# Sparse attention and a routed expert layer on one core: masks in another order, two stores moved, the last expert's pairs swapped, the fallback flag read earlier

## The chip, the cores and the metric

The kernel runs on 1 core of a Trainium2 chip. A time is the device time of one execution of the program in microseconds (us); a kernel's time is the median of its runs. The core has a matrix engine (PE; its weight loads are listed apart as PEld), a vector engine (DVE), a scalar engine (ACT), a general engine (POOL, which also issues the indirect DMAs here) and SyncE (SP, which issues the plain DMAs). Every engine works through its own instruction queue in order and waits on semaphores that the others raise.

## What is computed

An attention layer over 8 batches, 8 heads, 576 positions and head size 64, in float32, is followed by an expert layer on its output.

```python
mask_local = (rel >= 0) & (rel < 32)                       # heads 0 to 3
mask_strided = (rel >= 0) & (pos[None, :] % 32 == pos[:, None] % 32)   # heads 4 to 7
attn = softmax(where(mask, scale * q @ k.T, -1e9)); x = attn @ v       # (8, 576, 512)
...
logits = x @ w_gate                                        # 8 experts
for b in range(B):
    for s in range(S):                                     # fresh choice, or that of s - 1
        e = fresh_e if s == 0 or local_gate[b, s] < 0.5 else prev_e
        out[b, s] = p[e] * (relu(x[b, s] @ w1[e]) @ w2[e])   # 512 -> 1024 -> 512
```

## The kernel before, in words

The order of the work is written out by hand (`manual_schedule`): what the Python code emits first is first in each engine's queue.

**Attention** (`attention`, from line 143). A unit of work is a batch and a pair of heads; there are 32, in the order batch, then local pair, local pair, strided pair, strided pair. Each pair has two halves. A step n of the main loop emits for pair n the scores (PE, line 252) and the exponential (ACT, line 256), for local pairs the product with the mask `maskL` (DVE, line 263; strided pairs add their mask `maskS` by a matmul, line 246), and for pair n - 1 the product with the values (PE, line 276) and the normalization (DVE, lines 289 and 290). So in step n = 1 PE's queue holds the scores of pair 1 and behind them the values of pair 0. Before the loop all constants are made: `maskL` on POOL (lines 184 to 190), then in a loop over two sizes the two parts of `maskS`, the first 126 wide and the second 72 wide (lines 193 to 215: a chain of small DVE operations with some on POOL), then `fold`, `down`, `pos8` and `start` (lines 217 to 230). The first strided pair is pair 2. The list `also[n]` holds callables that are emitted at the end of step n.

**Routing** (`Router`). For batches 0 to 3 the choice of experts, the counts and the slot of each row are worked out during the attention, for batches 4 to 7 at the start of the expert stage. A row's number and its gate (8 bytes) are written to a table `slots` in DRAM by indirect DMAs on POOL, 20 for each half (`scatters`, line 577). `fetch` (line 643) reads the table back into `tab`, and `table` (line 647) makes the row numbers `gi`. `arms` also works out `pick`, for each expert which of 7 code arms it needs, and `flag` (line 676), which is positive when the fast path does not hold.

**Experts** (`Experts.run`). The rows of an expert are handled in pairs of tiles of 128 rows. A pair's first layer, `pair_hidden`, has 7 products of 16 matmuls (line 807; one level of a Strassen scheme, whose sums are on DVE, line 795). Its second layer, `pair_output`, has 7 products of 8 (line 843) and two indirect stores of 128 rows to `out`, `scatter` (line 763). `gather` (line 737) fetches the rows of a coming pair, `scale` and `turn` (lines 743, 750) multiply by the gate and transpose them, in the middle of the pair before. `steps` and `places` are lists of callables that `run(steps)` emits at marked points inside a pair; the first such point of `pair_hidden` lies behind its second product. The first two pairs (`self.first` of expert 0, `other` of expert 1) are known early. During the first one the second routing is emitted, whose 20 slot scatters stand in POOL's queue with the two stores of the first pair among them.

An expert may have more rows than its two pairs take. `choose(e)` (lines 960 to 965) loads `pick[e]` into a register of PE, ACT, DVE and POOL and gives a prefetch hint for the arms. `rest` runs the second pair of the expert up to the middle of its second layer, branches (`tc.Switch`, line 975), and finishes the pair in the arm, followed by the further tiles: none, a half tile of 64 rows (`half`, lines 919 to 941), a whole one (`single`, lines 898 to 910), both, and so on. For experts 1 and 0 `choose` stands ahead of the layer; for experts 2 to 7 it stands between the first pair's `pair_hidden` and its `output`. For expert 7 nothing follows the arm but the end.

**The end.** After the expert stage `values_load(flag)` (line 118) loads the flag into a register of all five engines, and `tc.If(redo > 0)` (line 120) holds a slow general version of the whole program, which is skipped on this input.

Part of `pair_output` with the stores that are moved:

```python
            def part2(nxt, steps):
                ...
                add(y[:, 1, 256:], v3, vb)
                self.scatter(y, 1, r)
                self.turn(nxt, bank)
                run(steps)
                ...
                add(y[:, 0, 256:], v4, va)
                self.scatter(y, 0, r)
```

Of the kernel before, what the change touches and what calls it, by code (L numbers as in the profile page):

```python
# [93 lines left out]
@with_exitstack  # L94
def attention_then_scomoe(ctx: ExitStack, tc: tile.TileContext, qkl, qks, vl, vs, wg, q, k, vl2, vs2, wg2, w1, w2, out):
    nc = tc.nc
    dram = ctx.enter_context(tc.tile_pool(name="dram", bufs=1, space=DRAM))
    xd = dram.tile([N, D], F32, name="xd")
    keep = ctx.enter_context(tc.tile_pool(name="keep", bufs=1))
    ident = keep.tile([P, P], F32, name="ident")  # L100
    make_identity(nc, ident)

    with ExitStack() as fast:
        once = fast.enter_context(tc.tile_pool(name="once", bufs=1))
        router = Router(once, dram, tc, ident)
        one = Weights(once)
        spot = (once.tile([P, 2, D], F32, name="x0"), once.tile([P, 2, DK, P], F32, name="xt"),
                once.tile([P, 4, 2, P], F32, name="tt"))
        with tc.manual_schedule():
            moe = Experts(nc, tc, xd, w1, w2, out, ident, router, one, spot)  # L110
            with ExitStack() as part:
                attention(part, tc, qkl, qks, vl, vs, wg, xd, ident, router, moe)
            with ExitStack() as part:
                moe.run(part)
        flag = router.flag


    redo = nc.values_load(flag, min_val=0, max_val=P + N,
                          skip_runtime_bounds_check_because="a count of at most 128 rows and of pairs")
    with tc.If(redo > 0):  # L120
        with ExitStack() as slow:
            general(slow, tc, q, k, vl2, vs2, wg2, w1, w2, xd, out, ident)

# [19 lines left out]
def attention(ctx, tc, qkl, qks, vl, vs, wg, xd, ident, router, moe):  # L143
# [46 lines left out]
    nc.gpsimd.memset(maskL[0:STRIDE, 0], 0.0)  # L190

    maskS = consts.tile([GK, 2 * GK + GL], BF16, name="maskS")
    for n, c in ((GK, GC), (GL, GR)):
        i = consts.tile([GK, n], I32, name=f"i{n}")
        cls = consts.tile([GK, n], F32, name=f"cls{n}")
        div = consts.tile([GK, n], F32, name=f"div{n}")
        both = []
        for mult, pattern in ((1, [[0, n]]), (0, [[1, n]])):

            nc.gpsimd.iota(i, pattern=pattern, base=0, channel_multiplier=mult)  # L200
            t = consts.tile([GK, n], F32, name=f"cls{n}{mult}")
            nc.vector.tensor_copy(t, i)
            nc.vector.tensor_scalar(i, i, 65536 // c + 1, None, Alu.mult)
            nc.vector.tensor_scalar(i, i, 16, None, Alu.arith_shift_right)
            nc.vector.tensor_copy(div, i)
            nc.vector.scalar_tensor_tensor(t, div, -float(c), t, Alu.mult, Alu.add)
            both.append(t)
        nc.vector.tensor_tensor(cls, both[0], both[1], op=Alu.not_equal)
        nc.vector.tensor_scalar(cls, cls, NEG, None, Alu.mult)
        nc.gpsimd.affine_select(out=cls, in_=cls, compare_op=Alu.is_ge, fill=NEG, base=0, pattern=[[1, n]],  # L210
                                channel_multiplier=-1)
        if n == GK:
            nc.vector.tensor_copy(maskS[:, 0:2 * n].rearrange("p (a x) -> p a x", a=2), across(cls, [n, 2, n]))
        else:
            nc.vector.tensor_copy(maskS[:, 2 * GK:], cls)

    fold = consts.tile([P, E + 1], F32, name="fold")
    nc.vector.tensor_reduce(fold, ident.rearrange("p (k x) -> p x k", k=DK)[:, 0:E + 1], axis=AX.X, op=Alu.add)


    ci = consts.tile([P, E], I32, name="ci")
    nc.gpsimd.iota(ci, pattern=[[-1, E]], base=E, channel_multiplier=0)
    down = consts.tile([P, E], F32, name="down")
    nc.vector.tensor_copy(down, ci)
    pi = consts.tile([P, CH], I32, name="pi")
    nc.gpsimd.iota(pi, pattern=[[E * P, CH]], base=E, channel_multiplier=E)
    pos8 = consts.tile([P, CH], F32, name="pos8")
    nc.vector.tensor_copy(pos8, pi)
    start = consts.tile([P, CH], F32, name="start")
    nc.vector.tensor_scalar(start, pos8, float(E), None, Alu.is_equal)  # L230

    def spans(u):

# [160 lines left out]
        u.n = n  # L394

    also = {n: [] for n in range(len(units) + 3)}
    also[2] = [router.constants]
    n = PAIRS * RB + 3
    turn, scan, hot, count, slot, back = router.steps(0, bank)
# [327 lines left out]
class Experts:  # L727
# [41 lines left out]
    def run(self, ctx):  # L769
# [66 lines left out]
        def pair_output(r, w, h):  # L836
# [25 lines left out]
                nc.scalar.copy(out=y[:, 0, 0:256], in_=va)  # L862
                run(steps)

            def part2(nxt, steps):
                self.scale(nxt)
                prod(k2, t[2], qb)
                add(v2, q1, vb)
# [17 lines left out]

# [65 lines left out]

            return [[todo.pop(0) for _ in range(min(n, len(todo)))] for n in counts]

        def output(r, w, h, nxt, steps):
            part1, part2 = pair_output(r, w, h)
            part1(steps)
            part2(nxt, steps)

        def choose(e):  # L960
            value = nc.values_load(router.pick[0:1, e:e + 1], engines=ENG, min_val=0, max_val=ARMS - 1,
# [2 lines left out]
            tc.switch_hint(index, ARMS, label=f"expert{e}")  # L964
            return index

        def rest(e, w, spot, second, index, steps, nxt):

            if nxt is not None:
                self.gather(nxt)  # L970
            part1, part2 = pair_output(second, w, pair_hidden(second, w, steps))
            part1(steps)
            flip = state["flip"]

            for arm in tc.Switch(index, ARMS, hint=f"expert{e}"):
# [22 lines left out]
                while left:  # L998
                    run(left)


        sums = load(1, W[1])
        other = Rows(spots[1], *self.early, [1, EARLY + 1], RB * S)
# [20 lines left out]
        index = choose(0)  # L1024
        sums = load(2, W[1])
        nxt = rows(0, 2, (0, 1))
        rest(0, W[0], 1, second, index, slots(sums, [0, 0, 1, 2, 1, 2, 2, 2, 2]) + [[f] for f in sums], nxt)
        for e in range(2, E):
            w, first, steps = W[(e + 1) % 2], nxt, []
            second = rows(1, e, (2, 3))  # L1030
            self.gather(second)
            if e + 1 < E:
                steps = slots(load(e + 1, W[e % 2]), [0] * 5 + [1, 1, 1, 3] + [1] * 8 + [2])
                nxt = rows(0, e + 1, (0, 1))
            else:
                nxt = None
# [3 lines left out]
            rest(e, w, 1, second, index, steps, nxt)  # L1040


def shifted_attention(ctx, tc, q, k, vl, vs, wg, xd, ident, probs, codes):
# [460 lines left out]
```

## Time and profile before

| | |
|---|---|
| runs | 739.37, 734.49, 740.71 us; median 739.37 |
| the profiled execution | 738.92 us, its span 737.2 us, mean granted TensorE clock 0.959 |
| busy, share of the span | PE 683.0 us (93%), PEld 586.5 (80%), DVE 353.4 (48%), ACT 195.5 (27%), POOL 134.7 (18%) |
| stages | attention 0 to about 199 us, first pair of the experts 199 to 229, pair `other` of expert 1 229 to 269, all others 269 to 725, end 725 to 737.2 |
| arm of expert 7 in this run | one whole tile and one half tile |

How to read it: the span is the time from the first instruction to the last. A line of the timeline has the start, the duration, the engine, the line of the kernel, the operation with its tiles, and in brackets how long the engine had been idle and what ended that. A line of the chain of waits has the start, the duration and what the end of the program waited for at that time; "issue" is time that nothing in the profile explains, "another core or an unknown queue" (in the timeline "remote") a wait that ended at a time at which no engine of the profile had just finished. `POOLq` and the like are rows of an engine's sequencer, such as branches and register loads, which do not count as busy.

### The profile page before, as it was taken

What the parts mean: (1) busy time and instruction counts of PE and PEld (TensorE: products, weight loads), DVE (VectorE), ACT (ScalarE), POOL (GpSimd) and SP (SyncE); (2) the same over time, 40 slices, a digit from 0 to 9 for tenths busy, and PEclk for the clock granted to TensorE, in tenths of its full rate; (3) what the DMA queues carried; (4) which work ended last, traced back from release to release, by engine and by line L of the source; (5) the groups of instructions that cost most, each with busy time, mean ns of one, the idle gap of its engine ahead of it and who ended that gap; (6) DMA issues with size and microseconds to landing.
All of it is one profiled execution on the core that took longest, in us unless ns stands there. A gap on an engine that the chain in (4) does not pass through costs nothing.

```text
span 737.2 us, 14832 instructions
## 1 busy us (share of the span) xinstructions
PE 683.0 (93%) x6034; PEld 586.5 (80%) x6034; DVE 353.4 (48%) x843; ACT 195.5 (27%) x357; POOL 134.7 (18%) x150
## 2 busy tenths in 40 slices
PE   7999999497899699999999999999999999999992
PEld 5878887385698589985998899999589899789961
DVE  6568766272466534451463265455126646524300
ACT  2544443141321122212222123122322222222210
POOL 3000001405127330221121120221012012111010
PEclk9999999597699899999999999999999999999997
DMA  9797887731360022615321711720171262010010
GB/s 325 275 328 267 279 286 256 249 84 52 95 228 30 3 86 67 238 38 173 109 74 47 254 47 50 251 73 21 39 257 59 76 210 66 32 37 30 18 50 13
DMA packets 37803, 95.33 MB, mean 129 GB/s; under 512 B 5230, under 2 KB 14446, under 8 KB 37632
## 3 DMA queue, kind: packets, MB, share of 16 engines
q1 hardware_dynamic: 29616, 73.77, 29.0%
q0 software_dynamic: 7488, 19.56, 8.4%
q8 instruction: 66, 1.08, 0.6%
q14 instruction: 105, 0.86, 0.4%
q10 hardware_dynamic: 528, 0.07, 0.1%
HBM read 74.41 MB, written 19.49 MB: 127 GB/s over the span
## 4 chain that ended last, share of the span: by engine, by line
PE 79%; issue 7%; DVE 5%; DMA 3%; another core or an unknown queue 3%; ACT 1%; POOL 1%; SPq 0%; DVEq 0%; POOLq 0%; ACTq 0%
PE mps L843 26%; PE lps L807 25%; PE vps L276 5%; PE sps L252 4%; PE tps L317 3%; PE lps L898 3%; PE mps L909 3%; PE xps L750 2%; DMA w1t<-in_w_dram 2%; PE mps L935 2%; PE lps L919 1%; PE sps L246 1%; PE tps L336 1%; PE vps L354 1%
## 5 line engine op out<-in xcount | busy, mean ns | idle before, releaser
L763 POOL DMA_INDIRECT out_dram<-y,tab x40 | 45.5, 1138 | 323.9 <-DVE y L795 217.4
L807 PE MATMUL lps<-tt,ws 128*128 128x128 f32 x768 | 91.5, 275 | 0.4 <-issue 0.2
L807 PEld LDWEIGHTS lps<-tt,ws 128*128 128x128 f32 x768 | 88.5, 192 | 0.8 <-DVE u L795 0.4
L843 PE MATMUL mps<-wt,k 128*128 128x256 f32 x384 | 85.6, 379 | 0.0
L843 PEld LDWEIGHTS mps<-wt,k 128*128 128x128 f32 x384 | 72.9, 190 | 9.9
L577 POOL DMA_INDIRECT slots<-tok,idx x40 | 40.9, 1023 | 147.5 <-DVE tok L568 135.9
L807 PE MATMUL lps<-xt,w1t 128*128 128x128 f32 x512 | 64.8, 281 | 2.6 <-ACT y L941 1.4
L807 PEld LDWEIGHTS lps<-xt,w1t 128*128 128x128 f32 x512 | 62.1, 196 | 6.1 <-ACT y L941 2.8
L795 DVE TENSOR_TENSOR h<-lps,u 128x512 f32<-128x512 f32 x48 | 33.2, 691 | 66.5 <-PE lps L807 57.3
L843 PE MATMUL mps<-w2t,h 128*128 128x256 f32 x256 | 61.3, 383 | 0.0
L737 POOL DMA_INDIRECT x<-xd,gi x40 | 40.4, 1009 | 112.5 <-PE lps L807 34.9
L252 PE MATMUL sps<-qk 64*128 64x96 f32 (+2 forms) x704 | 55.4, 288 | 4.9 <-issue 4.1
L252 PEld LDWEIGHTS sps<-qk 64*128 64x128 f32 (+2 forms) x704 | 45.5, 188 | 14.8 <-issue 12.5
L256 ACT ACTIVATE e<-sps 128x576 f32<-128x576 f32 (+1 forms) x64 | 41.2, 651 | 58.4 <-PE sps L252 40.8
L843 PEld LDWEIGHTS mps<-w2t,h 128*128 128x128 f32 x256 | 48.1, 193 | 6.0
L794 ACT ACTIVATE h<-h 128x512 f32<-128x512 f32 x48 | 30.3, 630 | 75.5 <-DVE h L795 71.7
L794 ACT ACTIVATE h<-lps 128x512 f32<-128x512 f32 x28 | 16.5, 594 | 86.8 <-PE lps L807 58.8
L795 DVE TENSOR_TENSOR u<-lps,p 128x512 f32<-128x512 f32 x16 | 11.1, 692 | 57.9 <-PE lps L807 32.3
L807 PE MATMUL lps<-xt,ws 128*128 128x128 f32 x256 | 33.1, 285 | 6.0 <-DVE h L795 6.0
L743 ACT ACTIVATE x<-x,tab 128x512 f32<-128x512 f32 (+1 forms) x40 | 27.2, 718 | 40.6 <-DMA x<-xd,gi 26.9
L807 PEld LDWEIGHTS lps<-xt,ws 128*128 128x128 f32 x256 | 31.5, 201 | 6.2 <-DVE h L795 6.2
L276 PE MATMUL vps<-vl,e 128*64 128x65 f32 x768 | 29.4, 235 | 7.0 <-issue 4.7
(222 smaller groups left out, 977.4 us busy)
## 6 DMA issues: line engine op xcount, KB each, us to landing
w1t<-in_w_dram SPq DMA_DIRECT2D x8, 2048.0 KB
w2t<-in_w_dram SPq DMA_DIRECT2D x8, 2048.0 KB
qk<-in_qkl_dram SPq DMA_DIRECT2D x16, 592.0 KB
qk<-in_qks_dram SPq DMA_DIRECT2D x16, 576.0 KB
vl<-in_vf_dram SPq DMA_DIRECT2D x8, 780.0 KB
vs<-in_vg_dram SPq DMA_DIRECT2D x8, 639.8 KB
xd<-xl SPq DMA_DIRECT2D x16, 288.0 KB
xd<-xs SPq DMA_DIRECT2D x64, 63.0 KB
```

Of the source, the lines that this page charges most:

```text
L252: nc.tensor.matmul(ps[0:m, h, c:c + w], lhsT=t[r, S + j * width:S + j * width + m], rhs=t[r, j * width:j * width + w], start=(u.local and ...
L256: nc.scalar.activation(e[0:kb, :, 0:n], ps[0:kb, :, 0:n], Act.Exp, bias=0.0, scale=1.0 / DH ** 0.5)
L276: nc.tensor.matmul(ps[a * HALF:(a + 1) * HALF, h, i], lhsT=u.e[0:m, h, q0:q0 + HALF], rhs=vt[0:m, j, 2 * i2 + h], start=(i == 0 and h == 0 ...
L317: nc.tensor.transpose(ps[:, t], src[:, t], ident)
L577: s = self.nc.gpsimd.indirect_dma_start(out=self.T, out_offset=bass.IndirectOffsetOnAxis(ap=self.idx[0:m, t, b:b + 1], axis=0), in_=self.t ...
L737: self.nc.gpsimd.indirect_dma_start(out=r.x[0:r.m, i], out_offset=None, in_=self.xd[0:r.rows], in_offset=bass.IndirectOffsetOnAxis(ap=r.gi ...
L743: self.nc.scalar.activation(r.x[0:r.m, i], r.x[0:r.m, i], Act.Copy, scale=r.gate[i][0:r.m])
L763: s = self.nc.gpsimd.indirect_dma_start(out=self.out, out_offset=bass.IndirectOffsetOnAxis(ap=r.si[i][0:r.m], axis=0), in_=y[0:r.m, i], in ...
L794: relu = lambda o, i: nc.scalar.activation(o, i, Act.Relu)
L795: add = lambda o, i, p: nc.vector.tensor_tensor(o, p, i, op=Alu.add)
L807: nc.tensor.matmul(ps[:, f], lhsT=m[:, kk, f * P:(f + 1) * P], rhs=v[:, kk], start=(start and f == 0 and kk == 0), stop=(kk == 1), skip_gr ...
L843: nc.tensor.matmul(ps[:, 0:256], lhsT=m[:, f], rhs=v[:, f], start=(start and f == 0), stop=(f == 3), skip_group_check=True)
```

## The change

- Only the first part of `maskS` is made ahead of the loop. The second part is emitted at the end of step 0, the other small constants at the end of step 1.
- The two stores of the first pair are kept in a list and emitted behind `router.fetch()`, so in POOL's queue behind all 20 slot scatters and the fetch.
- For experts 1, 0 and 7 `choose` becomes the first step inside `pair_hidden`, behind its second product.
- For expert 7 the pair with tiles 0 and 1 goes through `rest` (with the switch and the further tiles), and the pair with tiles 2 and 3 comes behind the switch.
- The flag is loaded inside the first layer of that last pair. The `If` has another block as its fall-through: in the program the empty branch now lies directly behind the compare, and the general version behind it is jumped over; before, the general version lay directly behind the compare and the empty branch behind that.

```diff
-        flag = router.flag
-    redo = nc.values_load(flag, min_val=0, max_val=P + N, ...)
-    with tc.If(redo > 0):
+                redo = moe.run(part)
+    with tc.If(redo > 0, preferred_fallthrough_block=False):
...
-    for n, c in ((GK, GC), (GL, GR)):
+    def classes(n, c):
...
+    classes(GK, GC)
     fold = consts.tile([P, E + 1], F32, name="fold")
-    nc.vector.tensor_reduce(fold, ...)
+    def more_constants():
+        nc.vector.tensor_reduce(fold, ...)
...
+    also[0] = [lambda: classes(GL, GR)]
+    also[1] = [more_constants]
     also[2] = [router.constants]
...
-            def part2(nxt, steps):
+            def part2(nxt, steps, late=None):
+                send = self.scatter if late is None else lambda *a: late.append(lambda: self.scatter(*a))
...
-                self.scatter(y, 1, r)
+                send(y, 1, r)
...
-                self.scatter(y, 0, r)
+                send(y, 0, r)
...
-        def rest(e, w, spot, second, index, steps, nxt):
-            if nxt is not None:
-                self.gather(nxt)
-            part1, part2 = pair_output(second, w, pair_hidden(second, w, steps))
+        def rest(e, w, spot, pair, steps, nxt, index=None):
+            self.gather(nxt)
+            if index is None:
+                steps = [[lambda: chosen.append(choose(e))]] + steps
+            part1, part2 = pair_output(pair, w, pair_hidden(pair, w, steps))
             part1(steps)
+            index = index or chosen.pop()
...
-        output(self.first, W[0], pair_hidden(self.first, W[0], places), other, places)
+        late = []
+        output(self.first, W[0], pair_hidden(self.first, W[0], places), other, places, late)
...
         router.fetch()
+        for do in late:
+            do()
         output(other, W[1], h, second, places)
...
-        rest(1, W[1], 0, second, choose(1), [], nxt)
+        rest(1, W[1], 0, second, [], nxt)
...
-        for e in range(2, E):
+        for e in range(2, E - 1):
...
+        second = rows(0, e + 1, (2, 3))
+        rest(e + 1, W[e % 2], 1, nxt, [], second)
+        check = lambda: chosen.append(nc.values_load(router.flag, ...))
+        output(second, W[e % 2], pair_hidden(second, W[e % 2], [[check]]), None, [])
+        return chosen.pop()
```

More of the change, by code (lines that the diff above doesn't have):

```diff
@@ L113, in attention_then_scomoe @@
             with ExitStack() as part:
-                moe.run(part)
-        flag = router.flag
-    redo = nc.values_load(flag, min_val=0, max_val=P + N,
-                          skip_runtime_bounds_check_because="a count of at most 128 rows and of pairs")
-    with tc.If(redo > 0):
+                redo = moe.run(part)
+    with tc.If(redo > 0, preferred_fallthrough_block=False):
         with ExitStack() as slow:
@@ L215, in attention @@
             nc.vector.tensor_copy(maskS[:, 2 * GK:], cls)
+    classes(GK, GC)
     fold = consts.tile([P, E + 1], F32, name="fold")
-    nc.vector.tensor_reduce(fold, ident.rearrange("p (k x) -> p x k", k=DK)[:, 0:E + 1], axis=AX.X, op=Alu.add)
     ci = consts.tile([P, E], I32, name="ci")
-    nc.gpsimd.iota(ci, pattern=[[-1, E]], base=E, channel_multiplier=0)
     down = consts.tile([P, E], F32, name="down")
-    nc.vector.tensor_copy(down, ci)
     pi = consts.tile([P, CH], I32, name="pi")
-    nc.gpsimd.iota(pi, pattern=[[E * P, CH]], base=E, channel_multiplier=E)
     pos8 = consts.tile([P, CH], F32, name="pos8")
-    nc.vector.tensor_copy(pos8, pi)
     start = consts.tile([P, CH], F32, name="start")
-    nc.vector.tensor_scalar(start, pos8, float(E), None, Alu.is_equal)
+    def more_constants():
+        nc.vector.tensor_reduce(fold, ident.rearrange("p (k x) -> p x k", k=DK)[:, 0:E + 1], axis=AX.X, op=Alu.add)
+        nc.gpsimd.iota(ci, pattern=[[-1, E]], base=E, channel_multiplier=0)
+        nc.vector.tensor_copy(down, ci)
+        nc.gpsimd.iota(pi, pattern=[[E * P, CH]], base=E, channel_multiplier=E)
+        nc.vector.tensor_copy(pos8, pi)
+        nc.vector.tensor_scalar(start, pos8, float(E), None, Alu.is_equal)
     def spans(u):
@@ L953, in slots, with output @@
             return [[todo.pop(0) for _ in range(min(n, len(todo)))] for n in counts]
-        def output(r, w, h, nxt, steps):
+        def output(r, w, h, nxt, steps, late=None):
             part1, part2 = pair_output(r, w, h)
             part1(steps)
-            part2(nxt, steps)
+            part2(nxt, steps, late)
         def choose(e):
@@ L999, in rest @@
                     run(left)
+        chosen = []
         sums = load(1, W[1])
@@ L1019, in run @@
         router.fetch()
+        for do in late:
+            do()
         output(other, W[1], h, second, places)
         nxt = rows(1, 0, (2, 3))
-        rest(1, W[1], 0, second, choose(1), [], nxt)
+        rest(1, W[1], 0, second, [], nxt)
         second = nxt
-        index = choose(0)
         sums = load(2, W[1])
         nxt = rows(0, 2, (0, 1))
-        rest(0, W[0], 1, second, index, slots(sums, [0, 0, 1, 2, 1, 2, 2, 2, 2]) + [[f] for f in sums], nxt)
-        for e in range(2, E):
-            w, first, steps = W[(e + 1) % 2], nxt, []
+        rest(0, W[0], 1, second, slots(sums, [0, 1, 2, 1, 2, 2, 2, 2]) + [[f] for f in sums], nxt)
+        for e in range(2, E - 1):
+            w, first = W[(e + 1) % 2], nxt
             second = rows(1, e, (2, 3))
             self.gather(second)
[L1032 to L1036, printed above, removed]
+            steps = slots(load(e + 1, W[e % 2]), [0] * 5 + [1, 1, 1, 3] + [1] * 8 + [2])
+            nxt = rows(0, e + 1, (0, 1))
             h = pair_hidden(first, w, steps)
@@ L1039, in run @@
             output(first, w, h, second, steps)
-            rest(e, w, 1, second, index, steps, nxt)
+            rest(e, w, 1, second, steps, nxt, index)
+        second = rows(0, e + 1, (2, 3))
+        rest(e + 1, W[e % 2], 1, nxt, [], second)
+        check = lambda: chosen.append(nc.values_load(
+            router.flag, min_val=0, max_val=P + N,
+            skip_runtime_bounds_check_because="a count of at most 128 rows and of pairs"))
+        output(second, W[e % 2], pair_hidden(second, W[e % 2], [[check]]), None, [])
+        return chosen.pop()
 def shifted_attention(ctx, tc, q, k, vl, vs, wg, xd, ident, probs, codes):
```

## The prediction

> **What bounds the kernel now.** I read the page first, then the table of stages (the busy time of each engine in chosen stretches), then for each place that the change touches the timeline, and for the end the sequencer's rows by line.
>
> ```profile
> span 737.2 us, 14832 instructions
> PE   7999999497899699999999999999999999999992
> PEclk9999999597699899999999999999999999999997
> ```
>
> PE is busy in nine tenths or more of most slices. What is left stands in a few places. The columns of the next view are the stretch, its length, then for each engine busy us and instructions, then the granted PE clock, the DMA share and GB/s.
>
> ```profile
> 8.40:11.80 3.40, 1.58 (x24) 1.45 (x24) 2.74 (x15) 1.38 (x3) 1.43 (x9) 1.00 1.06 307
> 11.80:15.20 3.40, 2.83 (x49) 2.71 (x49) 3.18 (x6) 0.00 (x0) 1.90 (x7) 0.50 0.99 370
> ...
> 126.00:143.00 17.00, 6.71 (x72) 4.88 (x70) 2.65 (x11) 0.62 (x3) 10.61 (x11) 0.65 0.80 244
> ...
> 170.00:199.00 29.00, 20.38 (x210) 15.56 (x211) 7.03 (x27) 7.56 (x15) 11.16 (x12) 0.71 0.30 80
> ...
> 243.10:249.00 5.90, 0.00 (x0) 0.00 (x0) 0.70 (x2) 0.15 (x1) 3.78 (x4) 0.86 0.02 1
> ...
> 247.30:254.10 6.80, 5.06 (x20) 4.79 (x21) 5.57 (x16) 1.26 (x2) 0.98 (x1) 0.50 0.06 8
> ...
> 700.00:737.00 37.00, 23.59 (x142) 14.88 (x140) 1.12 (x2) 4.01 (x9) 4.80 (x5) 0.89 0.10 32
> ```
>
> PE loses time at 8 to 15 us, in three stretches in which POOL is the busy engine (126 to 143, 170 to 199, 233 to 254), and at the end. Between 269 and 700 it is busy for 425.8 of 431 us, so little can be won there. The change touches the first, the last of the three stretches, and the end.
>
> **Part 1, masks.** In the timeline of the start:
>
> ```profile
> 8.50 1.58 PE L252 MATMUL sps<-qk 64*128 64x96 f32 x24 [0.72 <-ACT e L256]
> 11.57 2.76 DVE L263 TENSOR_TENSOR e<-e,maskL 128x576 f32<-128x576 f32 x4
> 12.37 2.87 PE L276 MATMUL vps<-vl,e 128*64 128x65 f32 x48 [2.29 <-DVE e L263]
> 17.35 0.87 PE L317 MATMUL tps<-ident,xl 128*128 128x128 f32 x6
> ```
>
> PE has done the scores of pair 1 at 10.08 and waits 2.29 for DVE, which works on the second mask (7.64 to 11.04) and small constants (to 11.57) before it masks pair 0, whose exponentials are ready at 8.48. After: DVE masks pair 0 by 9.2 (two operations of 0.7), so PE starts the values at 10.08, 2.29 earlier. What is late next: DVE makes the second mask from 9.2 to 12.6 (3.4, as before), masks pair 1 to 14.0, then does the four norm operations of pair 0 (0.2 and 0.56 each, 1.6 in all) to 15.6; PE's transposes, which began at 17.35, wait for those. Net 1.8 earlier. The small constants (0.6 on DVE) come next, ahead of the norm of pair 1, for which PE's values take 1.6 anyway. The second mask is done at 12.6 and PE needs it then for pair 2. On POOL the clearing of `sums` (0.46) moves ahead of two index rows that DVE takes at 9.2 or later: nothing. The loads follow PE's progress, and DMA is at 0.57 of its time from 27 to 36, so the shift should pass on. Bounds: 2.3 (the whole wait), and 0.1 if the new gap of about 1.6 before the transposes halves the clock for one stretch of 3.4 (1.7 lost). I take 1.8: PE is busy for more than 2 of the 3.4 us there, more than in the row 8.40:11.80, after which the clock halved.
>
> The Trainium skill's page "TensorE: Matmul & The Clock Gate", section "What's actually happening", puts the clock at half after an idle window of about 3.4 us. The rows above go against it in part: 1.58 busy of 3.40 was enough to halve it. By the page alone the gap of 1.6 costs nothing and the start gains 1.8 for certain; by the rows 0.1 stays possible.
>
> **Part 2, stores behind the slots.** The chain of waits and the timeline at the third stretch:
>
> ```profile
> 235.22 3.03 another core or an unknown queue
> 240.16 8.11 another core or an unknown queue
> ```
>
> ```profile
> 232.33 0.98 POOL L763 DMA_INDIRECT out_dram<-y,tab  x1 [0.31 <-issue]
> 245.77 0.92 POOL L577 DMA_INDIRECT slots<-tok,idx  x1 [0.30 <-issue]
> 248.08 0.98 POOL L643 DMA_DIRECT2D tab<-slots  x1 [1.40 <-DMA slots<-tok,idx]
> 248.30 0.69 DVE L795 TENSOR_TENSOR h<-lps,u 128x512 f32<-128x512 f32 x1 [8.13 <-remote]
> 249.04 3.78 PE L807 MATMUL lps<-xt,ws 128*128 128x128 f32 x16 [5.97 <-DVE h L795]
> ```
>
> DVE waits for a product whose matmuls began by 238.8, yet goes on at 248.30, 1.6 after POOL's last slot scatter (246.69). The two earlier stretches end alike: scatters end at 139.9 and 181.9, the engines go on at 142.5 and 183.1. So the profile ties the release to the end of the unbroken row of scatters; what holds PE's completions it does not show. The two stores stand in this row at 228.24 (1.17 and a pause of 0.30) and 232.33 (0.98 and 0.30). Without them the last scatter ends 2.75 earlier, and by the rule of the three stretches the release too. I take 2.75. The clock: PE works 249.0 to 254.1 at half, a loss of 2.5; with the idle stretch 2.75 shorter I expect one stretch of 3.4 at half, a loss of 1.7, so 0.8 more. What stands behind: the fetch goes out at 245.3, the stores end by 248.9, and the gathers behind them wait for DVE's `gi` (before: 259.79), so they are not held. `gi` needs the table, now read 2.75 earlier.
> Bounds: the pair's first layer took from 229.34 to 252.82, 23.5, where the next takes 12.5. If the stores cause the stretch (it sets in right behind them, and eight scatters from 216.2 to 228.2 held nobody), all 11.0 goes. If instead the release waits for the whole row of POOL's DMAs, now with the stores (to 248.9) behind the fetch, it comes at 250.5: 2.2 lost. The other two stretches had no stores among their scatters, which is why I stay with 2.75.
>
> **Part 3, choices inside the layer.** Before, DVE and ACT come back from expert 1's arm at 300.2 and 298.1, load the register (0.33 and 0.39) and then work on a product that is ready; PE waits 0.21 for DVE at 301.7. After, the load (with its hint 0.9) stands behind that work, ahead of `u3`, which PE needs two products later (3.6). Gain 0.2. Bounds: 0.6 (13.1 from 294.4 to 307.5 against 12.5), and 1.0 lost if PE's own load (0.32, with its hint 0.96) drains its queue in the middle of a layer; the nearest row, between two layers, shows no gap, hence 0.2. The flag's load is one such row (0.3) per engine and as well covered.
>
> **Part 4, the end.** The sequencer's rows of POOL, by line (name, times in ns, first and last start in us):
>
> ```profile
> L118 POOLq TENSOR_LOAD <-flag x1: 312/312/312, 730.2 to 730.2; - x1
> L120 POOLq EVENT_SEMAPHORE  x5: 17/42/43, 733.3 to 733.6; - x5
> L120 POOLq INC_SWDGE_SEM  x1: 642/642/642, 733.7 to 733.7; - x1
> L1500 POOLq COMPARE_BRANCH  x1: 45/45/45, 726.6 to 726.6; - x1
> ```
>
> PE ends at 725.07. The last store starts at 726.16; POOL leaves the arm at 726.7 and has its next instruction at 730.2: 3.55 for the jump. Flag 0.4, jump over the general version 2.6 (to 733.3), waits for the stores 0.4, queue count 0.64, then 2.8 to 737.2. From the store's start: 11.04.
> After: no arm to leave, no flag to load. But the empty branch now comes before the jump: the wait for the store's landing (2.7 after its start for 128 rows: 702.32 to 705.04) is no longer beside it. From the store's start: 2.7 + 0.4 + 0.64 + jump 2.6 + 2.8 = 9.2. From PE's end to that start: one DVE sum 0.42 and 0.3 instead of two ACT copies, 0.75 for 1.09. Tail 2.2 shorter.
> In PE's work the same matmuls stand. The half tile's gap of 0.70 at 719.3 is filled by the next pair's transposes, as at 643.9 (1.02, against 0.87 where they stood). The gap of 0.79 stays. New is one join: PE waits 0.47 after a half tile (650.3, 537.3), and the layer behind it takes 12.77 or 13.1 for 12.5, since ACT and DVE come back late; 0.74 to 1.07. Net 0.3 lost; part 4 gains 1.9. Bounds: 3.7 (the landing is beside the jump after all) and 0.3 lost (a join whose returns cost the whole 2.2 more; the slowest return, POOL's 6.3, does not hold PE).
>
> **The sum.** 1.8 + 2.75 + 0.8 + 0.2 + 1.9 = 7.45. From the profiled execution's 738.92: 731.5. That execution lies 0.45 below the median of 739.37. A measurement of this kernel tells about 1% from no change.
>
> **The rivals.**
> A, the stores cause the third stretch: 11.0 instead of 3.55, so 738.92 - 1.8 - 11.0 - 0.2 - 1.9 = 724.0. For it: the onset right behind the stores. Against: the two other stretches.
> B, the release waits for POOL's whole row of DMAs: 2.2 lost instead of 3.55 won, 737.2. For it: gathers (169.5 and 170.8) stand ahead of the second stretch, so it need not be the 8-byte scatters alone. Against: POOL pauses 1.4 for the landing before the fetch, and before, the release came in that pause.
> C, slower: the join behind expert 7's arms. If the code pages of the engines come one behind the other (1.7 + 5.3 + 5.8 + 6.0 = 18.8 from the rows at 291 to 303) PE waits some 13.8 more than now (ACT's return matters from about 5 on), 745.3 or more. It makes the kernel slower from a return of 12.4 on. Against: seven joins of the profile, none above 6.3.
>
> **How the numbers follow.** The forecast (728.5 to 734.5) has 0.53, A 0.17, B 0.22, C 0.08. Faster by over 1% is below 732.0: all of A and 0.33 of the forecast, 0.50. Slower by over 1% is above 746.8: most of C, 0.06. The rest, 0.44, lies within 1%. The range takes A and B in: 722 to 738.5 leaves out the lower end of A and C.
>
> **What would show it.** Right: PE's values at 10.1; DVE's product behind the scatters some 2.7 earlier against its pair's start, the two stores behind the fetch; no POOL jump of 3.5 behind the last store, and its queue count before the last jump. Wrong: half clock between 15 and 19; PE idle until the stores are out (B) or not at all (A); ACT or DVE more than 6 us away after expert 7's arm.

## The result, and the profile after

In a comparison of 20 executions each on the same chips the changed kernel takes 733.18 us (730.52 to 739.49) and the kernel before 737.24 (732.62 to 741.38). The ratio is 0.9945, with a 95% interval of 0.9925 to 0.9966: 4.1 us gained (2.5 to 5.5), where the prediction summed up 7.45. The profiled execution of the changed kernel took 733.33 us, 5.6 less than that of the kernel before.

The head of its page, and the table of stages (stretch, its length, busy us and instructions of PE, PEld, DVE, ACT and POOL, granted PE clock, DMA share, GB/s):

```profile
span 731.5 us, 14839 instructions
PE   8999998597898899999999999999999999999993
PEclk9999999597799799999999999999999999999998
```

```profile
8.40:11.80 3.40, 3.39 (x74) 3.10 (x74) 3.07 (x13) 1.42 (x3) 0.19 (x1) 1.00 1.06 315
11.80:15.20 3.40, 2.39 (x26) 1.71 (x25) 2.94 (x9) 1.30 (x2) 2.72 (x13) 1.00 1.02 384
126.00:143.00 17.00, 7.95 (x71) 5.13 (x74) 4.52 (x14) 1.79 (x4) 8.11 (x9) 0.56 0.84 242
170.00:199.00 29.00, 22.21 (x181) 17.45 (x182) 9.78 (x41) 7.16 (x15) 8.66 (x9) 0.66 0.24 64
231.00:237.10 6.10, 3.54 (x26) 3.05 (x25) 1.89 (x3) 0.00 (x0) 4.86 (x5) 1.00 0.02 1
237.10:247.40 10.30, 7.98 (x35) 7.56 (x35) 4.69 (x8) 1.50 (x3) 6.07 (x6) 0.50 0.18 57
```

The start has changed: PE is busy for all of 8.4 to 11.8, and the stretch behind it runs at full clock (from 15.2 to 18.6 too, with PE busy for 3.32 of 3.40). The two stretches of the attention are there as before. So is the third: PE works 3.54 of 6.10 us from 231, and then it is at half clock for 10.3 us, where it was 6.8 before.

The timeline of the start:

```profile
7.88 1.43 DVE L263 TENSOR_TENSOR e<-e,maskL 128x576 f32<-128x576 f32 x2
9.92 1.62 PE L276 MATMUL vps<-vl,e 128*64 128x65 f32 x48
12.42 0.20 DVE L212 CAST maskS<-cls 126x72 bf16<-126x72 f32 x1 [0.35 <-POOL cls L207]
12.54 1.42 DVE L263 TENSOR_TENSOR e<-e,maskL 128x576 f32<-128x576 f32 x2
14.80 1.15 PE L317 MATMUL tps<-ident,xl 128*128 128x128 f32 x6 [0.87 <-DVE sums L289]
```

DVE masks pair 0 at once, PE's values start at 9.92 (12.37 before), the second mask is done at 12.62, and the transposes begin at 14.80 (17.35).

The third stretch, where `other` (expert 1's first pair) begins at 226.02. "Release" is the time at which the engines behind PE go on again:

```profile
234.06 0.69 DVE L797 TENSOR_TENSOR u<-lps,p 128x512 f32<-128x512 f32 x1 [6.15 <-remote]
239.06 0.91 POOL L579 DMA_INDIRECT slots<-tok,idx  x1 [0.30 <-issue]
241.35 0.97 POOL L645 DMA_DIRECT2D tab<-slots  x1 [1.39 <-DMA slots<-tok,idx]
241.84 0.69 DVE L797 TENSOR_TENSOR u<-lps,u 128x512 f32<-128x512 f32 x1 [5.88 <-remote]
242.59 3.77 PE L809 MATMUL lps<-tt,w1t 128*128 128x128 f32 x16
242.63 1.37 POOL L765 DMA_INDIRECT out_dram<-y,tab  x1 [0.30 <-DVE u L797]
244.31 1.47 POOL L765 DMA_INDIRECT out_dram<-y,tab  x1 [0.30 <-issue]
246.16 2.53 PE L809 MATMUL lps<-xt,ws 128*128 128x128 f32 x16
```

The last scatter ends at 239.97 and the engines go on at 241.84, before the two stores are out. So the release has come 6.5 us earlier, 3.1 of it against the start of its pair. But DVE had already waited 6.15 for the sum before, and PE still has two products to do behind the release, both slowed by the half clock (3.77 and 2.53). Before, it had one.

The end, POOL's sequencer rows at the last store (it starts at 721.61) and behind it, by line (name, shortest, median and longest in ns, first and last start):

```profile
L117 POOLq EVENT_SEMAPHORE  x5: 17/43/3267, 721.5 to 721.8; - x5
L117 POOLq COMPARE_BRANCH  x2: 48/54/60, 721.4 to 725.8; - x2
L117 POOLq INC_SWDGE_SEM  x1: 635/635/635, 725.1 to 725.1; - x1
```

```profile
L1514 POOLq DRAIN  x3: 44/112/2039, 728.6 to 731.3; - x3
```

No jump stands behind the last store any more: the compare is at 721.4, 3.27 us go into the wait for the landing, then the queue count, and only then the second branch (725.8), behind which nothing comes until 728.6.

Where the 5.7 us between the two spans lie, read from the start times of the same matmuls in both: 2.27 at the start, 1.05 at a wait before the transposes at 54.40, 0.42 in pair `other`, 0.67 in the layer behind expert 1's arm, 0.26 in small pieces, 0.44 at expert 7's choice, 0.40 lost at its join, 0.97 behind PE's end. The wait of 0.99 at 54.40 belongs to none of the parts for certain: the kernel with the masks alone (below) still has it, the one with the choices alone does not.

### The profile page after: what moved, and what is told of

The parts are those of the page before. It is cut to its first block, busy times and chain, and to the rows that moved or that the text cites. A ratio compares the mean times of both kernels' runs of the same rounds, so it can differ in the third digit from the quotient of the medians.

```text
span 731.5 us, 14839 instructions
## 1 busy us (share of the span) xinstructions
PE 683.5 (93%) x6034; PEld 586.7 (80%) x6034; DVE 353.2 (48%) x843; ACT 195.4 (27%) x357; POOL 134.6 (18%) x150
## 5 line engine op out<-in xcount | busy, mean ns | idle before, releaser
L809 PE MATMUL lps<-tt,ws 128*128 128x128 f32 x768 | 93.6, 277 | 3.8 <-issue 3.8
L809 PEld LDWEIGHTS lps<-tt,ws 128*128 128x128 f32 x768 | 90.1, 194 | 5.0 <-issue 4.2
L579 POOL DMA_INDIRECT slots<-tok,idx x40 | 40.6, 1015 | 143.1 <-DVE tok L570 131.5
L797 DVE TENSOR_TENSOR u<-lps,p 128x512 f32<-128x512 f32 x16 | 11.1, 692 | 65.0 <-PE lps L809 27.9
L809 PE MATMUL lps<-tt,w1t 128*128 128x128 f32 x256 | 33.1, 285 | 0.0
L753 ACT COPY xt<-xps 128x512 f32<-128x512 f32 (+1 forms) x38 | 20.0, 564 | 45.6 <-PE xps L752 45.5
```

The source lines that it names most:

```text
L579: s = self.nc.gpsimd.indirect_dma_start(out=self.T, out_offset=bass.IndirectOffsetOnAxis(ap=self.idx[0:m, t, b:b + 1], axis=0), in_=self.t ...
L753: self.nc.scalar.copy(out=r.xt[:, i, :, 0:r.m], in_=ps[:, :, 0:r.m])
L797: add = lambda o, i, p: nc.vector.tensor_tensor(o, p, i, op=Alu.add)
L809: nc.tensor.matmul(ps[:, f], lhsT=m[:, kk, f * P:(f + 1) * P], rhs=v[:, kk], start=(start and f == 0 and kk == 0), stop=(kk == 1), skip_gr ...
```

## The experiments

Times are medians, and ratios are to runs of the kernel before, taken beside them on the same chip.

### Each part by itself

`masks`: the masks' part of the change on the kernel before.

```diff
+    classes(GK, GC)
...
+    also[0] = [lambda: classes(GL, GR)]
+    also[1] = [more_constants]
```

> The kernel before with the masks' part of the change alone. Prediction: PE starts the values of pair 0 at 10.1 instead of 12.37, 1.8 us gained in the end. Theory from the trace of the whole change: 2.3 us at the start (no half clock from 11.8 to 15.2, a gap of 0.9 before the first transposes), and 1.0 more at 54, where PE waited 0.99 for DVE before and does not after: 3.3 us in all. Rival: the lead is lost again in the stretches in which POOL works through its rows of scatters, since these start by the routing, not by PE; then less than 1 us, and the lead shrinks in the trace at 126 to 150 or at 170 to 190.

736.30 us, ratio 0.9981 (0.9950 to 1.0013). In its trace the values of pair 0 start at 9.99 and the lead at 19.3 us is 2.34, as in the whole change. Of the time between this point and 117, 0.8 us more pass than in the profile of before; that stretch differs by up to 3.6 us between the profiles of all kernels. Where pair `other` begins, 0.9 of the lead is left (228.48 for 229.34), as the rival had it; with that spread one profile does not decide. So the start gains what the theory said; that it all reaches the end these times cannot show.

`stores`: the two stores moved behind the fetch, nothing else.

```diff
-                self.scatter(y, 1, r)
+                send(y, 1, r)
...
         router.fetch()
+        for do in late:
+            do()
```

> The kernel before with the two stores moved behind the fetch, nothing else. Prediction: the last slot scatter ends 2.75 us earlier, the engines are released with it, and PE works less at half clock: 3.55 us gained. Theory from the trace of the whole change: the row does end about 3 us earlier against the start of the pair, but without the store at 228.24 and its wait the row has no pause, PE's completions stop sooner (at the third product of the pair instead of the fifth), and PE has two products more to do behind the release: 0.3 to 1 us gained. Rival A (the stores cause the stretch): 11 us. Another rival: the half clock lasts longer than before, and nothing is gained or up to 2 us lost.

738.03 us, ratio 1.0006 (0.9977 to 1.0035). Its timeline in the third stretch, pair `other` beginning at 232.19:

```profile
244.81 0.91 POOL L577 DMA_INDIRECT slots<-tok,idx  x1 [0.30 <-issue]
246.18 0.69 DVE L795 TENSOR_TENSOR u<-lps,p 128x512 f32<-128x512 f32 x1 [12.09 <-remote]
247.12 0.98 POOL L643 DMA_DIRECT2D tab<-slots  x1 [1.39 <-DMA slots<-tok,idx]
250.51 0.69 DVE L795 TENSOR_TENSOR u<-lps,u 128x512 f32<-128x512 f32 x1 [2.45 <-remote]
```

The row ends 13.5 us after the pair's start instead of 17.3, the release follows it, and nothing is won: DVE gets its first sum, which it had at 4.0 us in the profile of before, only with the release, after 12.09 us. The hidden layer (the pair's first layer, from its first product to the start of the second layer) takes 24.6 us, where it took 23.3 in the kernel before. It is neither 3.55 nor 11: the interval leaves room for a gain of 1.7 at most.

`choices`: the choices of experts 1 and 0 inside the layer.

```diff
-        rest(1, W[1], 0, second, choose(1), [], nxt)
+        rest(1, W[1], 0, second, None, [], nxt)
...
+            if index is None:
+                steps = [[lambda: chosen.append(choose(e))]] + steps
```

> The kernel before with the choices of experts 1 and 0 loaded inside the first layer, nothing else. Prediction: 0.2 us gained. Theory from the trace of the whole change: 0.67 us gained between 294 and 304, where the layer behind expert 1's arm took 13.1 and takes 12.5. Rival: loading in the middle of a layer drains PE's queue, 0 to 1 us lost. None of it is beyond what the times can tell; the trace has to.

738.66 us, ratio 1.0015 (0.9986 to 1.0043). The layer behind expert 1's arm, PE's rows:

```profile
298.05 1.95 PE L807 MATMUL lps<-xt,w1t 128*128 128x128 f32 x16
299.84 1.95 PE L807 MATMUL lps<-tt,ws 128*128 128x128 f32 x16
```

No gap stands between these two, the fourth and the fifth product (0.21 before), and the layer takes 12.50 us. In the four profiles with the choice ahead of the layer it takes 12.84 to 13.17 (mean 13.0). That is 0.5 gained there; the times cannot tell it from nothing.

`end`: the last expert's pairs, its choice, the flag and the fall-through.

```diff
+        rest(e + 1, W[e % 2], 1, nxt, [], second)
...
+        output(second, W[e % 2], pair_hidden(second, W[e % 2], [[check]]), None, [])
...
+    with tc.If(redo > 0, preferred_fallthrough_block=False):
```

> The kernel before with the last expert's pairs swapped, its choice and the flag loaded inside a layer, and the other fall-through of the If; masks, stores and the choices of experts 1 and 0 as before. Prediction: 1.9 us gained (2.2 in the tail, 0.3 lost in PE's work). Theory from the trace of the whole change: the tail from PE's end to the end of the program goes from 12.1 to 11.1, 1.0 us, and PE's work gains or loses 0.1. The tail is worth less than forecast since POOL's jump and what stands behind the landing come one after the other. Rival: the join behind expert 7's arms costs more than it does in the trace, 0 us gained.

737.51 us, ratio 1.0002 (0.9971 to 1.0033). PE's end to the program's end is 11.34 us. `masks`, `stores` and `choices`, which have the old end, show 11.58, 11.66 and 11.50, and in them POOL's jump out of the arm takes 2.5 to 2.6: the 3.55 in the profile of before was an unusually long one. POOL's rows of `end`:

```profile
L117 POOLq EVENT_SEMAPHORE  x5: 17/43/3625, 729.0 to 729.4; - x5
```

The landing is waited for 3.63 here (3.27 in the changed kernel). Expert 7's choice inside the layer gains 0.44 (84.91 for 85.35 us in the stretch that ends at 674.8 in the profile of before), the join behind its arm loses 0.40 (50.67 for 50.27 from there to PE's end), to the same hundredth in `end` and in the changed kernel.

### One part undone

`after_no_stores` is the changed kernel with the two stores back in their old places.

```diff
-        output(self.first, W[0], pair_hidden(self.first, W[0], places), other, places, late)
+        output(self.first, W[0], pair_hidden(self.first, W[0], places), other, places)
...
-        for do in late:
-            do()
```

> The changed kernel with the two stores back in their old places, all else as changed. Prediction (stores behind the slots are worth 3.55): 3.55 us slower than the changed kernel. Theory from the runs so far (the row's end and PE's stop move together, so nothing is won): within 1 us of the changed kernel; the time from the first hidden product of pair other to the first of the next pair stays between 39 and 40.5 us (39.4 in the kernel before, 38.96 in the changed one, 40.9 with the stores alone). Rival: the stores' move loses, and the kernel is 1 to 2 us faster than the changed one.

734.28 us, ratio 0.9977 (0.9943 to 1.0010), where the changed kernel had 0.9945 in its own comparison. The two intervals overlap, and they would also leave room for 3.55 us, so the times settle nothing here; `stores` above excludes 3.55 us, and the traces show why. The pair takes 40.6, just above what the theory allowed.

With this the third stretch can be laid side by side for eight profiles. "Sums" are DVE's sums of pair `other` that were through before the release; the times count from the start of the pair, in us.

| profile | stores in the row, and POOL's pause of 0.7 | row ends | release | sums | hidden layer | whole pair |
|---|---|---|---|---|---|---|
| before | yes | 17.3 | 19.0 | 2 | 23.3 | 39.4 |
| masks | yes | 17.6 | 19.3 | 2 | 23.6 | 39.7 |
| choices | yes | 17.6 | 19.3 | 2 | 23.6 | 39.4 |
| end | yes | 17.4 | 18.6 | 2 | 22.9 | 41.8 |
| after_no_stores | yes | 17.3 | 18.2 | 2 | 22.5 | 40.6 |
| changed kernel | no | 14.0 | 15.8 | 1 | 22.5 | 39.0 |
| stores | no | 13.5 | 14.0 | 0 | 24.6 | 40.9 |
| after_old_jump (below) | no | 14.0 | 15.8 | 1 | 21.3 | 38.1 |

The row ends 3.6 us earlier without the stores, the release comes 3.7 earlier, and one or two sums fewer are through by then. The hidden layer is 0.4 us shorter on average (22.8 for 23.2), the pair 0.8 (39.3 for 40.2), with a spread of 2.4 to 2.8 us in the pair within each kind. With `free_tick` (below; 24.0 and 40.3), whose row has neither stores nor a wait, the two differences are 0.1 and 0.6. What the stores had brought is seen in the second column: the first of them waited 0.7 us for its sum, just before the pair began. In the kernel before:

```profile
228.24 1.17 POOL L763 DMA_INDIRECT out_dram<-y,tab  x1 [0.69 <-DVE y L795]
233.32 0.69 DVE L795 TENSOR_TENSOR u<-lps,p 128x512 f32<-128x512 f32 x1 [2.09 <-PE lps L807]
238.27 0.69 DVE L795 TENSOR_TENSOR u<-lps,u 128x512 f32<-128x512 f32 x1 [3.05 <-remote]
```

In all five profiles with this pause DVE got its first sum 4.0 to 4.8 us into the pair and a second one, still before the release, at 7.7 to 9.2. Without it the row of 20 scatters is unbroken and the first sum comes after 8.0 to 14.0 us. In this table the stores and the pause always come together, so it cannot part the two; what a pause does without stores, the gates below test.

`after_old_jump` is the changed kernel with the old order of the blocks.

```diff
-    with tc.If(redo > 0, preferred_fallthrough_block=False):
+    with tc.If(redo > 0):
```

> The changed kernel without the new fall-through: the general version lies directly behind the compare again and is jumped over at the compare; the flag is still loaded early. Theory from the rows of the end (the jump of 2.8 now stands behind the landing and the queue count, in a row; with the old order it stood beside the landing): PE's end to the program's end falls from 11.1 to about 8.3 us, the kernel is 2.8 us faster than the changed one. Rival (the other fall-through saves a jump, and the 2.8 behind the count comes in any case): the same time or up to 3 us slower, with 2.6 for the jump and 2.8 behind the count.

731.03 us, ratio 0.9921 (0.9890 to 0.9952). POOL's rows at its end:

```profile
L117 POOLq EVENT_SEMAPHORE  x5: 17/43/106, 725.3 to 725.6; - x5
L117 POOLq COMPARE_BRANCH  x1: 69/69/69, 722.3 to 722.3; - x1
L117 POOLq INC_SWDGE_SEM  x1: 639/639/639, 725.8 to 725.8; - x1
```

One compare instead of two. The jump (3.0 us from 722.3 to 725.3) now lies beside the landing, of which 0.1 is left to wait for, and the end follows the queue count directly. From PE's end to the program's end it is 7.99 us, 3.2 less than in the changed kernel (11.15) and 3.6 less than in `masks`, `stores` and `choices`. So the early flag and the swapped pairs were worth 3.6 us, and the other fall-through gave 3.2 of it back. The step from 0.9945 to 0.9921 is only 1.8 us, and the two intervals are wide enough for 3.2 as for nothing, so it is the traces that show the 3.2.

### What holds PE in the third stretch

`gate_other` puts four small copies on POOL into the row, each of an element that DVE or ACT makes from PE's products.

```diff
+        def gate(t):
+            nc.gpsimd.tensor_copy(tick, t)
...
-        for place in places:
-            place += [more.pop(0) for _ in range(2)]
+        for place, n in zip(places, ("u2", "h11", "h22", "h21")):
+            place += [lambda n=n: gate(kept[n][0:1, 0, 0:1])] + [more.pop(0) for _ in range(2)]
```

> The changed kernel with POOL held four times in its row of slot scatters: before each two of the last eight, POOL copies one element of a sum that DVE or ACT makes from the pair's products (u2, h11, h22, h21), so it goes on only as PE does. Theory 1 (PE's completions are held while POOL issues its DMAs without a pause, and a pause lets them through): no wait of 6 to 8 us for a product, the hidden layer of pair other takes 12.5 to 16 us instead of 22.5, and pair other 29 to 33 instead of 39; the kernel is 6 to 10 us faster than the changed one. Theory 2 (each scatter costs the PE beside it a fixed time, or the DMA engines are full): the waits are spread but the hidden layer still takes 20 us or more; no gain, or a loss of 1 to 3 us, since the row ends later.

727.00 us, ratio 0.9890 (0.9842 to 0.9937). The hidden layer takes 12.50 us, with no wait for a product; theory 2 falls. The pair takes 32.9, since its second layer now waits 3.42 for the rows that the table names.

`free_tick` has the four copies read a constant, so that they wait for nothing; `one_gate` has only the first gate. Against the changed kernel:

```diff
+        for place in places:
+            place += [lambda: nc.gpsimd.tensor_copy(tick, self.ident[0:1, 0:1])] + [more.pop(0) for _ in range(2)]
```

```diff
+        places[0].insert(2, lambda: gate(kept["u2"][0:1, 0, 0:1]))
```

> As gate_other, but the four copies on POOL read a constant and so wait for nothing: the row of scatters has four small instructions in it (0.5 us each) and no wait. Theory 1 (what lets PE's completions through is a pause in which POOL issues nothing): PE stops as in the changed kernel, the hidden layer of pair other takes 21 us or more. Theory 3 (any POOL instruction between the scatters that is not a DMA does it): 12.5 to 14 us, as in gate_other, and the row ends 2 us earlier than there.

> As gate_other with the first of the four gates alone (before the last eight scatters POOL waits for u2, a pause of about 2 us). Theory 1, one pause clears what had gathered in the twelve scatters before it, and eight scatters behind it (10 us) are too few to stop PE for long: the hidden layer takes 12.5 to 15 us. Theory 1b, each stretch of more than some 6 us of scatters beside the hidden layer stops PE again: 15 to 20 us. Theory 2 (a price for each scatter): 22 us.

`free_tick`: 734.56 us, ratio 0.9953 (0.9925 to 0.9980), hidden layer 23.97. `one_gate`: 725.04 us, ratio 0.9849 (0.9805 to 0.9893), hidden layer 12.50, pair 32.1. The timelines, `free_tick` first:

```profile
230.03 0.18 POOL L1024 COPY tick<-ident 1x1 f32<-1x1 f32 x1
230.38 0.99 POOL L579 DMA_INDIRECT slots<-tok,idx  x1 [0.17 <-issue]
239.34 0.91 POOL L579 DMA_INDIRECT slots<-tok,idx  x1 [0.30 <-issue]
241.97 0.69 DVE L797 TENSOR_TENSOR u<-lps,p 128x512 f32<-128x512 f32 x1 [13.45 <-remote]
```

```profile
227.82 0.98 POOL L579 DMA_INDIRECT slots<-tok,idx  x1 [0.31 <-issue]
230.84 0.57 POOL L1010 COPY tick<-u 1x1 f32<-1x1 f32 x1 [2.05 <-DVE u L797]
231.58 1.26 POOL L579 DMA_INDIRECT slots<-tok,idx  x1 [0.16 <-issue]
231.89 0.68 DVE L797 TENSOR_TENSOR u<-lps,u 128x512 f32<-128x512 f32 x1
241.90 0.91 POOL L579 DMA_INDIRECT slots<-tok,idx  x1 [0.30 <-issue]
```

Both kernels issue the same 20 scatters. In the first POOL goes from one to the next, with copies of 0.18 between, and DVE waits 13.45 us for its first sum, until behind the last of them. In the second there is one pause of 2.8 us before the last eight; the first sum comes 4.7 us into the pair, and PE has no gap in the layer. So the number of scatters does not decide. A break of 2.8 us in the row, in which POOL waits for a sum of PE's product, lets the products through, and four copies of 0.18 us that wait for nothing do not.

`long_tick` was to tell whether POOL has to wait, or whether 2 us of other work do as well.

```diff
+        places[0].insert(2, lambda: nc.gpsimd.memset(idle, 0.0))
```

> The changed kernel with one POOL instruction before the last eight scatters that waits for nothing and takes about 2 us (a memset of 128 x 2048 to a tile that nobody reads; 576 columns took 0.58 us). one_gate had a pause of 2.8 us there in which POOL waited for PE's product, and the hidden layer of pair other took 12.50 us; free_tick had copies of 0.18 us that waited for nothing, and it took 23.97. Theory 1 (the time without a DMA counts, whatever POOL does in it): 12.5 to 14 us, and 5 to 7 us faster than the changed kernel. Theory 4 (POOL has to wait for PE, so that PE's completions are what it goes on by): 20 us or more, no gain.

697.05 us, ratio 0.9923 (0.9894 to 0.9952), hidden layer 12.50. But this run tells nothing about the question: it fell on a chip on which the kernel before takes 702.46 us, and there the stretches of the attention, which `long_tick` leaves as they were, are absent too. So it stays open.

### The same in the attention, and all together

`gate_all` holds the first routing's 20 scatters as well, each behind the sums of a half pair that PE has just made.

```diff
+    def gate(n):
+        u = units[min(n, len(units)) - 1][i_half[0] % 2]
+        i_half[0] += 1
+        nc.gpsimd.tensor_copy(tick, sums[0:1, u.n, 0, 0:1])
...
-        also[m + i // 2].append(do)
+        also[m + i // 2] += [lambda n=m + i // 2: gate(n), do]
```

> As gate_other, and the 20 slot scatters of the first routing in the attention are held too: before each of them POOL copies one element of the sums of the half pair whose values PE has just made, so that about two scatters go out in a step of 6 us. Theory 1: the stretches at 126 to 145 and 170 to 186 go as well, with their half clock; a further 10 to 20 us are gained over gate_other. Theory 2: no gain over the changed kernel. If only some is gained, the scatters that still stand two in a row, or the fetches of the first rows behind them, hold PE for a shorter time.

716.04 us, ratio 0.9732 (0.9693 to 0.9771): 11 us better than `gate_other`. The first stretch in the kernel before, then two stretches of `gate_all`; the second had PE busy for 20.4 at a clock of 0.71 in the kernel before:

```profile
117.50:148.00 30.50, 20.21 (x239) 15.58 (x240) 11.09 (x37) 6.02 (x13) 11.65 (x12) 0.67 0.72 222
```

```profile
117.50:148.00 30.50, 28.75 (x518) 24.43 (x514) 22.27 (x86) 12.38 (x24) 12.14 (x20) 1.00 0.81 253
170.00:199.00 29.00, 23.76 (x175) 20.85 (x176) 13.33 (x37) 8.23 (x17) 5.72 (x9) 0.82 0.53 183
```

The first stretch of the attention is gone, with its half clock. In the second, waits of 3.0 and 3.9 us are left, where the last eight scatters and two fetches of rows still stand close together.

`best` takes what had helped: the old fall-through, all gates with the last four scatters of the first routing in the first pair's layer, and the two stores behind the fetch of the second pair's rows.

```diff
+    for i in range(16):
+        also[m + i // 2] += [lambda n=m + i // 2, g=i % 2: gate(n, g), todo.pop(0)]
...
+        for i, n in enumerate(("u2", "h11", "h22", "h21")):
+            places[i][0:0] = [lambda n=n: gate(kept[n][0:1, 0, 0:1]), self.left.pop(0)]
...
+        places += [[lambda: next(arms), router.table, lambda: self.gather(second)] + late]
```

> The changed kernel with what the runs so far speak for: the old fall-through (2.8 to 3.1 us), the gates of pair other, the first routing's scatters held to two in a step with the last four in the first layer of the first pair, and the two stores behind the fetch of the second pair's rows. gate_all measured 716.0; the fall-through gives 3, the stretch at 167 to 180 that was left there (two waits of 3 to 4 us) 3 to 7 us, the rows' fetch 0.7 us earlier: 705 to 710 us. If the scatters in the first pair's layer hold PE there instead, 711 to 714.

709.88 us, ratio 0.9627 (0.9588 to 0.9666): 27.6 us faster than the kernel before, and by the two ratios some 23 faster than the changed one. From PE's end it takes 8.03. One wait of 4.7 us at 173 is left, behind two scatters and two fetches in a row (166.3 to 171.1), and one of 2.7 at 237 for the second pair's rows.

## Why the prediction was partly wrong

The direction was right and the time lies in the range given (731.5; 722 to 738.5), but the gain was 4.1 and not 7.45. That 731.5 lies as near to 733.18 as it does is in part luck: the sum started from a profiled execution of 738.92, 1.7 above the median of 737.24. By its steps:

**Part 1, forecast 1.8, measured 2.3 (2.6 over all profiles).** The order was as foreseen: values at 10.1 (9.92), second mask done at 12.6 (12.62). The transposes came at 14.80 and not at 15.6, since the first of them need only the first half's sums, so the new gap is 0.87 and not 1.6. The clock's risk did not come in: behind the row 11.80:15.20 (2.39 busy of 3.40) the clock stays at 1.00. The Trainium skill's page "TensorE: Matmul & The Clock Gate", section "What's actually happening", by whose idle window of about 3.4 us this gap costs nothing, agrees here. In the four profiles without this part (`before`, `stores`, `choices`, `end`) PE's wait of 2.1 to 2.3 us, shorter than that window, is followed by half clock each time, for 3.4 us or more, so there the page's rule does not hold; in the ten with it the start stays at full clock. So the gain differs with the profile: the first matmul with the strided mask for pair 3 starts at 19.7 to 21.4 without the part and at 17.4 to 18.5 with it, 2.6 earlier on average.

**Part 2, forecast 2.75, measured 0 to 1: the step that failed.** "Without them the last scatter ends 2.75 earlier, and by the rule of the three stretches the release too": both happened, by 3.6 and 3.7. What was wrong is the silent step behind it, that an earlier release is an earlier end. It holds only if PE has done as much by then. PE stops sooner in the row without the stores, and has more to do behind the release. The pause stood in the timeline of before (POOL idle for 0.69 ahead of the store at 228.24), and the prediction gave it no part. `one_gate` shows that a pause of 2.8 us lets PE's completions through; that the one of 0.7 did so too, for two sums, rests on the table of eight profiles, where the stores themselves are not ruled out. The clue was in the kernel before: this pause, behind eight scatters, and then 7 us without a hold, to the first wait of the chain at 235.22. It is not the whole account: in the changed kernel, too, the row held nobody in its first 17 us (212.9 to 230.0), so the length of the row alone does not say when the hold sets in.

**The clock, forecast 0.8 gained.** The half clock lasted 10.3 us instead of 6.8, with PE at work in it for 7.98 us where it was 5.06: a loss of about 4.0 for 2.5, so 1.5 lost in this profile. It follows from the same step, since the work left behind the release falls into the half clock.

**Part 3, forecast 0.2, measured 0.5.** Within its bounds; the wait and the stretched matmuls of the layer both went.

**Part 4, forecast 1.9, measured 0.7.** PE's work did as foreseen: 0.40 lost at the join, 0.44 won by the choice inside the layer, which the prediction had not priced. Mis-sized was the tail, forecast 2.2 shorter. Old ends take 11.50 to 12.12 (mean of four 11.7), new ones 10.86 to 11.34 (mean of seven, `long_tick` left out, 11.1): 0.6. The arm's jump of 3.55 is 2.5 in three of four profiles; the last store starts 1.24 behind PE's end and not 0.75; the wait for its landing ends 3.4 to 3.8 behind that start, where 3.1 was taken, the 2.7 of a store in the middle of the kernel and 0.4 for the semaphores. That the landing and the jump now stand one behind the other was right, and it is the whole reason why so little came of it: `after_old_jump` has them side by side and gains 3.2 more.

**Rivals.** A falls: the stretch comes with no store among the scatters. B falls: the release came at 241.84, before the first store went out. C falls: behind expert 7's arms PE waits 0.47. A fourth case was missing, that the release comes earlier and PE stops earlier with it; with nothing for it in the sum the gain would have been 3.9 (1.8, 0.2 and 1.9), beside the 4.1 measured. That these lie so close is luck: parts 1 and 3 gained 1.1 more than forecast and part 4 1.2 less.

By the means over profiles the parts are 2.6, 0.8, 0.5 and 0.7, 4.6 in all, beside 4.1 (2.5 to 5.5) in the medians. The second of them is smaller than the spread between profiles.

## What to carry to other kernels

When a wait ends at a fixed event, ask not only when that event comes but how much the waiting engine gets done before it; moving the event earlier can move the stop earlier as well. Where a row of indirect DMAs without a pause holds another engine, it is worth breaking up by a wait on that engine, even where that makes the row longer (here the hidden layer fell from 22.5 to 12.5 us). And a jump that cannot be avoided belongs beside the wait for the last landing, not behind it.

## What the runs showed of the hardware

- While POOL issues a row of indirect DMAs without a pause (mostly one DMA each 1.28 us), the engines that work on PE's products come to wait for them, DVE for up to 13.45 us in the third stretch (`free_tick`), and PE's matmuls there come one to four at a time with gaps of 0.2 to 1.1 us. One wait of 2.8 us in the row lets them through. What it is that is held, the profile does not name.
- The length of the row does not say when it holds an engine: the changed kernel's row of 20 ran for 17 us before the first sum was late, and in `best` two scatters and two fetches from 166.3 to 171.1 were enough for a wait of 4.7 us. What makes the difference, no run here shows.
- It depends on the chip, or on something else that differed in that run: in `long_tick`, 12 scatters stand in a row as long as ever, and PE is busy all the time.

```profile
123.87 1.04 POOL L579 DMA_INDIRECT slots<-tok,idx  x1 [107.92 <-DVE tok L570]
...
138.27 0.97 POOL L579 DMA_INDIRECT slots<-tok,idx  x1 [0.30 <-issue]
```

```profile
117.50:148.00 30.50, 30.22 (x536) 26.06 (x534) 23.71 (x90) 14.48 (x27) 12.02 (x12) 0.97 0.79 244
```

  There the kernel before takes 702.46 us instead of 735 to 739. Why, no run here shows.
- A jump out of an expert's arm or past the general version takes POOL 2.5 to 3.6 us in these runs, and the jump out of expert 7's arm alone varies by 1 us between four profiles (2.5 to 3.55).
